# Moving one transform behind the sines, two products behind the next unit, and the last evictions onto two engines, in a kernel of attention and a state-space convolution

## The chip, the core and the metric

The kernel runs on one core of one Trainium2 chip. The core has a matrix engine (TensorE, PE in the profile, whose weight loads are listed as PEld), a vector engine (VectorE, DVE), an engine for casts and functions such as sine and exp (ScalarE, ACT), a general engine (GpSimd, POOL) and one that mostly issues DMAs (SyncE, SP). Each works through its own queue in order, and they wait for each other on semaphores. The metric is the device time of one execution in microseconds (us). The kernel before takes 423.83 us (median of 3 runs, 423.25 to 425.2).

## What is computed

There are two independent halves, whose results stand side by side in an output of 2048 x 1280.

```
a: qkv = x @ wqkv            x 2048 x 640, 32 heads of 20
   logits[s, w] = q[s] . k[s - 2w] * 20**-0.5,   w = 0..7   (window of 8, dilation 2)
   a = softmax_w(logits) applied to v[s - 2w], then @ wo
b: K[d, l] = Re sum_n C[d,n] * exp(dt[d] * A[d,n] * l) * dt[d] * B[d,n]     d 640, n 192, l 2048
   y = irfft( rfft(u padded to 4096) * rfft(K padded to 4096) )[:2048]      per channel d
   b = y + u * Dskip
```

In the second half, A is complex, so the exponential is a real exponential times a cosine and a sine of angles.

## The kernel before, in words

The 640 channels of b are worked through in five chunks of 128 (c = 0 to 4, `NCH`), in the first loop of `body`. For a chunk ScalarE makes tables of real exponentials (`exps_chunk`, 40 activations, tile R) and, in two halves of the chunk, tables of sines (`trig_half`: TensorE makes phases in the PSUM tiles ps_ph, ScalarE evicts them as sines into TA and TX, 8 evictions for a half). VectorE multiplies them together for each half (`small_half`: tiles PG, Q and two X) and then, for each of the two units of a half, makes three large product tables Y (`y_form`). TensorE contracts Y with X over n (`kgen_unit`, PSUM tile ps_k) and ScalarE evicts the unit's part of K into Ksb. Y has four buffers, which Q shares, so a new Y can be written only when the matmuls of an older one are done. A chunk has two halves of two units, so 12 Y in all.

The convolution is done in the frequency domain. `fwd` is a forward transform in two steps of 64 matmuls each: the first step's results are cast by ScalarE in four pieces into A, the second step's in four pieces into Sg. It is called as `transform(c)` for K of a chunk, and as `fwd_u` for u, whose spectrum goes to DRAM (Sdram). `products` loads the spectrum of u twice (P1, and P2 with its halves exchanged) and multiplies both by K's spectrum on VectorE (line 379). `inverse_a` is the first inverse step: four pieces of matmuls (ps_ia) and casts into Z, then a store to Zdram. A, Sg, P1, P2 and Z of both transforms share three buffers in turn (tag "sp"). All PSUM tiles of these steps (ps_ph, ps_f, ps_ia) share three double banks (tag "bank2"). `times_d` multiplies u with Dskip (tile UD) after certain units.

Chunk c works on the spectral steps of chunk c - 1: it runs transform(c - 1), then the two sets of sines, its first half's units, products and the inverse of c - 1, u's transform for chunk c + 1, and its second half, during which the exponentials and first sines of chunk c + 1 are made. In the last chunk, projections of q and k for the attention take the free places. Then the attention follows: products, logits and softmax, and `av_step`, which multiplies v by the attention weights on VectorE and sums over channels on TensorE (ps_o); at its last window position ScalarE evicts the two ps_o tiles into o. `out_proj` returns eight pieces for each quarter q of the rows; each piece is five matmuls into ps_op, an eviction into ob, and after every second piece a DMA to the output.

The order on each engine is made by a planner, from the order of the program as priorities and its own times for instructions. Two calls tie it down. `keep_in_program_order(ins)` places an instruction behind the one traced just before it on its engine. `issue_after(ins)` places all instructions that a block traces on the engine of `ins` behind `ins`. In chunks 1 to 4 the second half's `small_half` is placed in this way behind the second product of `products`, and the products of chunks 1 to 4 are kept in program order.

## Time and profile before

| what | value |
|---|---|
| median of 3 runs | 423.83 us |
| the profiled execution, its own time | 423.71 us |
| its span, first to last instruction | 421.9 us |
| busy: TensorE, VectorE, ScalarE | 352.2, 378.0, 313.6 us |
| mean granted TensorE clock | 0.935 of full speed |
| Y products, line 324, 60 of them | 103.1 us, 1753 ns each |
| casts of the first and second transform step, 40 each | 37.8 and 37.7 us |
| the chain that ended last | the last 8 projection pieces: PE 5.96 us, then one eviction of 0.49 us |

A row of the profile's timeline gives the start, the length of a run of like instructions, engine and line, operation, output and input tiles with their shapes, how many there were, and in brackets how long the engine had stood idle before them and which engine's instruction ended that. A row of the waits names who waited, for whom, the total in us, the number of times and the longest. A row of a table of stretches gives the stretch, its length, and the busy time of TensorE, the weight loads, VectorE, ScalarE and GpSimd with their numbers of instructions, then the granted clock, the share of DMA time and the rate in GB/s. Lines 441 and 442 are helpers through which all matmuls and copies of the attention's end go.

### The profile page before, as it was taken

The numbers are of one execution on the slowest core, as the hardware profiler recorded it, in microseconds if no ns is written. First come the engines' busy times: TensorE is split into PE (matmuls) and PEld (weight loads), VectorE is DVE, ScalarE is ACT, GpSimd is POOL, SyncE is SP. The second block draws the span as 40 slices with busy tenths as digits, with TensorE's granted clock in tenths as the row PEclk, the third lists the DMA queues.
The fourth block names the chain that finished last, engine by engine and source line by source line (L and its number), as shares of the span: only waits on it lengthen the run. The fifth ranks groups of instructions, "written<-read, shape, count | busy, mean of one in ns | idle before, by whom it ended". The sixth has DMA issues, their size and how long they took to land. (4 is left out here: it accounts for less than half of the span.)

```text
span 421.9 us, 18968 instructions
## 1 busy us (share of the span) xinstructions
PE 352.2 (83%) x8693; PEld 259.8 (62%) x8693; DVE 378.0 (90%) x350; ACT 313.6 (74%) x578; POOL 42.9 (10%) x85
## 2 busy tenths in 40 slices
PE   1288779989987888878997799999899989879895
PEld 0267678877865678666785586555545666445453
DVE  8999997998988999899996989955987999999961
ACT  2988989889998999979998684423666644746662
POOL 8630000000000000000010000000000300412120
PEclk9975969989997999889897899999999999999999
DMA  5599003262233402424079941700040472897642
GB/s 146 177 223 170 5 2 129 90 202 68 101 149 108 101 30 103 167 89 103 28 272 216 247 106 42 281 3 3 2 101 2 141 148 80 240 228 227 174 117 90
DMA packets 45336, 51.76 MB, mean 123 GB/s; under 512 B 31488, under 2 KB 39168, under 8 KB 42568
## 3 DMA queue, kind: packets, MB, share of 16 engines
q1 hardware_dynamic: 41592, 41.35, 36.4%
q0 software_dynamic: 3520, 9.08, 7.2%
q8 instruction: 68, 1.11, 1.1%
q10 hardware_dynamic: 144, 0.12, 0.1%
q14 instruction: 12, 0.10, 0.1%
HBM read 28.08 MB, written 18.35 MB: 110 GB/s over the span
## 5 line engine op out<-in xcount | busy, mean ns | idle before, releaser
L324 DVE TENSOR_TENSOR Y<-PG 128x3072 bf16<-128x3072 bf16 x60 | 103.1, 1753 | 6.8 <-PE ps_k L342 6.6
L337 PE MATMUL ps_k<-Y,X 128*32 128x64 bf16 x1920 | 47.6, 239 | 9.7 <-issue 6.5
L270 PE MATMUL ps_ph<-LPC 128*64 128x256 bf16 x400 | 44.4, 323 | 13.4 <-DMA LPC<-lo 8.7
L342 PE MATMUL ps_k<-Y,X 64*32 64x64 bf16 x1920 | 44.9, 234 | 4.6 <-issue 4.6
L337 PEld LDWEIGHTS <-X 128*32 128x32 bf16 x1920 | 32.2, 117 | 20.0 <-issue 12.5
L365 ACT CAST Sg<-ps_f 128x1024 bf16<-128x1024 f32 x40 | 37.7, 1042 | 7.7 <-PE ps_f L364 7.7
L244 ACT ACTIVATE R<-LPC 128x192 bf16<-128x192 f32 x155 | 41.8, 389 | 0.0
L357 ACT CAST A<-ps_f 128x1024 bf16<-128x1024 f32 x40 | 37.8, 1038 | 1.2 <-PE ps_f L356 1.1
L342 PEld LDWEIGHTS <-X 64*32 64x32 bf16 x1920 | 30.0, 113 | 13.8 <-issue 6.4
L294 DVE TENSOR_TENSOR X<-R,TX 128x1536 bf16<-128x1536 bf16 x40 | 37.2, 952 | 0.0
L364 PE MATMUL ps_f<-A,T 128*64 128x128 bf16 x640 | 25.3, 244 | 12.5 <-ACT A L357 10.5
L270 PEld LDWEIGHTS <-LPC 128*64 128x64 bf16 x400 | 21.5, 121 | 19.8 <-DMA LPC<-hi 8.8
L278 ACT ACTIVATE TX<-ps_ph 128x768 bf16<-128x768 int16 x40 | 30.4, 838 | 3.2 <-PE ps_ph L274 3.2
L364 PEld LDWEIGHTS <-T 128*64 128x64 bf16 x640 | 23.6, 127 | 14.3 <-issue 14.1
L630 DVE TENSOR_TENSOR prod<-v,atp 128x2048 bf16<-128x2048 bf16 (+2 forms) x32 | 30.8, 1018 | 0.7 <-PE ps_o L441 0.7
L274 PE MATMUL ps_ph<-LPC 128*64 128x128 bf16 x400 | 30.7, 249 | 0.0
L278 ACT ACTIVATE TA<-ps_ph 128x768 bf16<-128x768 int16 x40 | 29.8, 824 | 0.9 <-PE ps_ph L274 0.8
L274 PEld LDWEIGHTS <-LPC 128*64 128x64 bf16 x400 | 25.8, 131 | 1.1
L441 PE MATMUL ps_op<-wo,o 128*128 128x320 bf16 x160 | 23.9, 299 | 1.8 <-ACT ysb L442 0.9
L294 DVE TENSOR_TENSOR PG<-R,TA 128x3072 bf16<-128x3072 bf16 x10 | 17.5, 1752 | 8.0 <-ACT TA L278 8.0
L379 DVE TENSOR_TENSOR P<-P,Sg 128x4096 bf16<-128x4096 bf16 x10 | 22.9, 2287 | 2.0 <-DMA P<-Sdram 1.6
L543 DVE TENSOR_TENSOR prod<-qT,kT 128x1024 bf16<-128x1024 bf16 (+1 forms) x16 | 23.0, 1482 | 0.5 <-ACT qT L511 0.5
(135 smaller groups left out, 667.3 us busy)
## 6 DMA issues: line engine op xcount, KB each, us to landing
Sdram<-Sg SPq DMA_DIRECT2D x5, 1024.0 KB
P<-Sdram SPq DMA_DIRECT2D x5, 1024.0 KB
P<-Sdram SPq DMA_DIRECT2D x10, 512.0 KB
Zdram<-Z SPq DMA_DIRECT2D x5, 1024.0 KB
Z<-Zdram SPq DMA_DIRECT2D x30, 128.0 KB
U<-in_B_u_dram SPq DMA_DIRECT2D x4, 640.0 KB
UDdram<-UD SPq DMA_DIRECT2D x10, 256.0 KB
out_dram<-ysb SPq DMA_DIRECT2D x32, 80.0 KB
```

Source lines behind the costliest of these rows:

```text
L244: nc.scalar.activation(out=RX[:, :, e - 16, :], in_=src, func=ACT.Exp, scale=m)
L270: MM(o[64 * hh:64 * hh + 64, :, 0:8], lhsT=L[:, 64 * hh:64 * hh + 64], rhs=rhs, start=first, stop=last, skip_group_check=True, tile_positi ...
L274: MM(o[64 * hh:64 * hh + 64, :, 8:12], lhsT=L[:, 128:192], rhs=rhs[:, :, 16 * hh:16 * hh + 16], start=False, stop=last, skip_group_check=T ...
L278: last = nc.scalar.activation(out=dst, in_=words.rearrange("p b (q e f) -> p b q (e f)", e=8, f=4), func=ACT.Sin, scale=PI_LO / 32768.0)
L294: TT = lambda o, a, b, op: V.tensor_tensor(out=o, in0=a, in1=b, op=op)
L324: nc.vector.tensor_tensor(out=Y[:].rearrange("p q (b a) f -> p q b a f", a=8), in0=fa, in1=gb, op=A.mult)
L337: MM(ps[32 * g:32 * g + 32, t], lhsT=X[:, q, k, :, f], rhs=Ys[k][:, q, :, f], start=(t == 0 and k == 0), stop=False, tile_position=(0, 32 ...
L342: MM(ps[32 * g:32 * g + 32, t], lhsT=X[hb, q, k, :, f], rhs=Ys[k][hb, q, :, f], start=False, stop=(k == 2), tile_position=(64 * (g // 2), ...
L357: nc.scalar.copy(out=A1[:, :, 32 * b:32 * b + 32].rearrange("p k (j g) -> p k j g", g=4), in_=ps[:].rearrange("p j k g -> p k j g"))
L364: last = MM(ps[sl, kk], lhsT=C["T2"][:, 8 * b + kk, sl], rhs=A1[:, 8 * b + kk, :], start=(kk % 4 == 0), stop=True, skip_group_check=True, ...
L365: nc.scalar.copy(out=Sg[:, :, 8 * b:8 * b + 8, :], in_=ps[:].rearrange("p k (j g) -> p j k g", g=4))
L630: ins = nc.vector.tensor_tensor(out=p2.rearrange("p (d i) -> p d i", i=ni), in0=self.v2[:, 4 * j0:4 * j0 + 4 * nj, off:off + ni], in1=at[: ...
```

## The change

Four places of the program are edited.

- `fwd_u` for chunk c + 1 is called in chunks 1, 2 and 3 after the first sines of chunk c + 1, where it was called before the second half of chunk c. In chunk 0 it stays where it was.
- `products` and all four pieces of `inverse_a` are called after the second unit of the first half. Before, the products and the inverse's first piece stood between the two units and the other three pieces behind the second.
- The last `av_step` evicts its two ps_o tiles in four pieces, ScalarE and VectorE taking one half of each, where ScalarE took two whole ones.
- The last two pieces of the third quarter's projection are evicted by VectorE, and their store goes over SP. In the last quarter every second piece is evicted by VectorE as before, now tied to the program's order, and five of its eight pieces take PSUM from the double banks.

```diff
-    def av_step(self, i0, ni, j0, nj, w):
+    def av_step(self, i0, ni, j0, nj, w, last=False):
...
             for f, p in enumerate(self.ops):
-                self.copy(out=self.o4[:, j0:j0 + nj, 2 * f:2 * f + 2, i0:i0 + ni], in_=p[:, :, 0:n].rearrange("p s (j i) -> p j s i", i=ni))
+                for s in range(2) if last else ():
+                    (self.copy, self.vcopy)[s](out=self.o4[:, j0:j0 + nj, 2 * f + s, i0:i0 + ni], in_=p[:, s, 0:n].rearrange("p (j i) -> p j i", i=ni))
+                if not last:
+                    self.copy(out=self.o4[:, j0:j0 + nj, 2 * f:2 * f + 2, i0:i0 + ni], in_=p[:, :, 0:n].rearrange("p s (j i) -> p j s i", i=ni))
+
+    def vcopy(self, out, in_):
+        self.tc.keep_in_program_order(self.nc.vector.tensor_copy(out=out, in_=in_))
...
-        ps = self.one("ps_op")[:, 0:320]
+        if wide:
+            ps = self.big("ps_ow")[:, 0, 0:320] if (2 * sc + eh) % 5 < 3 else self.one("ps_op")[:, 0:320]
+        else:
+            ps = self.one("ps_op")[:, 0:320]
...
-            nc.vector.tensor_copy(out=ob[:, 320 * eh:320 * eh + 320], in_=ps)
+            self.vcopy(out=ob[:, 320 * eh:320 * eh + 320], in_=ps)
...
-        return [(lambda sc=sc, eh=eh: self.out_piece(q, sc, eh, last and eh == 1)) for sc in range(4) for eh in range(2)]
+        return [(lambda sc=sc, eh=eh: self.out_piece(q, sc, eh, eh == 1 if last else q == 2 and sc == 3, last)) for sc in range(4) for eh in range(2)]
...
         unit(c, 0, 0, F, G, Xs[0])
+        unit(c, 0, 1, F, G, Xs[1])
         if c > 0:
             P1, P2, last = products(tc, pools, Sk[c - 1], Sd[c - 1], fp, True)
-            ia = inverse_a(tc, pools, C, P1, P2, Zd[c - 1], fp)
-            ia[0]()
-        unit(c, 0, 1, F, G, Xs[1])
-        if c > 0:
-            for f in ia[1:]:
+            for f in inverse_a(tc, pools, C, P1, P2, Zd[c - 1], fp):
                 f()
-        if c < LAST:
-            last_u = fwd_u(tc, pools, C, Sd, c if c == 0 else c + 1)
-            if c == 0:
-                first_u = last_u
+        if c == 0:
+            first_u = fwd_u(tc, pools, C, Sd, 0)
...
             trig[c + 1, 0] = trig_half(tc, pools, B, c + 1, 0)
+            if c > 0:
+                fwd_u(tc, pools, C, Sd, c + 1)
...
-            att.av_step(i0, ni, j0, nj, w)
+            att.av_step(i0, ni, j0, nj, w, 8 * group + w == 47)
```

More of the change, by code (lines that the diff above doesn't have):

```diff
@@ L640, in av_step, with out_piece @@
             for f, p in enumerate(self.ops):
-                self.copy(out=self.o4[:, j0:j0 + nj, 2 * f:2 * f + 2, i0:i0 + ni], in_=p[:, :, 0:n].rearrange("p s (j i) -> p j s i", i=ni))
-    def out_piece(self, q, sc, eh, vec):
+                for s in range(2) if last else ():
[4 more added lines that the diff above has]
+        self.tc.keep_in_program_order(self.nc.vector.tensor_copy(out=out, in_=in_))
+    def out_piece(self, q, sc, eh, vec, wide=False):
         nc = self.nc
```

## The prediction

> **What bounds the kernel now.** I read the engines' shares first, then the stretches from one chunk's first VectorE instruction to the next one's, then the waits, then the timelines of VectorE, ScalarE, TensorE and the SP queue around them, and last the end of the run.
>
> ```profile
> PE 352.2 (83%) x8693; PEld 259.8 (62%) x8693; DVE 378.0 (90%) x350; ACT 313.6 (74%) x578; POOL 42.9 (10%) x85
> ...
> 74.30:128.05 53.75, 48.44 (x1521) 41.34 (x1519) 49.07 (x40) 50.41 (x95) 0.62 (x2) 0.94 0.37 124
> 128.05:178.04 49.99, 41.86 (x1214) 34.66 (x1210) 48.93 (x39) 47.25 (x92) 0.62 (x2) 0.94 0.28 96
> 178.04:230.05 52.01, 43.61 (x1280) 35.76 (x1278) 47.84 (x39) 47.46 (x91) 1.77 (x2) 0.89 0.52 147
> ...
> DVE PG L294 <- ACT TA L278: 8.0, 3, 4.0
> DVE Y L324 <- PE ps_k L342: 6.6, 4, 2.5
> ```
>
> VectorE leads, but the columns of the stretches of chunks 1, 2 and 3 (length, then TensorE, weight loads, VectorE, ScalarE) show three engines close together: 48.93 us of VectorE and 47.25 of ScalarE in a chunk of 49.99, and 41.86 of TensorE. A wait taken from one engine can go only as far as the next one lets it. VectorE's waits there are of two kinds: the new chunk's first product waits for the sines (8.0 us in three chunk changes), and the table product Y waits until TensorE has freed one of four Y buffers.
>
> ```profile
> 88.00 5.10 DVE L324 TENSOR_TENSOR Y<-PG 128x3072 bf16<-128x3072 bf16 x3
> 93.01 2.29 DVE L379 TENSOR_TENSOR P<-P,Sg 128x4096 bf16<-128x4096 bf16 x1
> 97.09 1.76 DVE L324 TENSOR_TENSOR Y<-PG 128x3072 bf16<-128x3072 bf16 x1 [1.78 <-PE ps_k L342]
> ...
> 128.05 1.76 DVE L294 TENSOR_TENSOR PG<-R,TA 128x3072 bf16<-128x3072 bf16 x1 [2.90 <-ACT TA L278]
> ```
>
> ```profile
> 108.33 3.80 ACT L357 CAST A<-ps_f 128x1024 bf16<-128x1024 f32 x4
> ...
> 112.97 3.76 ACT L365 CAST Sg<-ps_f 128x1024 bf16<-128x1024 f32 x4
> ...
> 125.05 2.92 ACT L278 ACTIVATE TA<-ps_ph 128x768 bf16<-128x768 int16 x4
> ...
> 132.87 3.80 ACT L357 CAST A<-ps_f 128x1024 bf16<-128x1024 f32 x4
> ```
>
> The first block shows both waits of chunk 1, and that the first spectral product P (2.2 us from start to start) fills part of the second. The second block is ScalarE: the casts of u's transform (108.33 and 112.97, about 7.5 us) stand ahead of the sines at 125.05, so the sines are 7.5 us later than they need be. The four casts at 132.87 begin the transform of the previous chunk's K. These casts stand at 82.86, 132.87, 183.91 and 236.38; I call them the anchors of chunks 1 to 4.
>
> **Part 1, u's transform behind the sines.** Nothing is added: 64 + 64 matmuls, 8 casts and one store of 1 MB move, once in each of chunks 1, 2 and 3. Before it, the sines come about 7.5 us sooner, against waits of 2.90, 1.06 and 4.04, so all 8.0 us of waiting for sines goes. That is the upper end. What is late next: the 8 casts now stand between the sines and the casts of K's transform, and the 128 matmuls among the six Y products' matmuls of the chunk's second half.
>
> **Part 2, products behind the second unit.** The two P are now tied behind the last Y of the first half (and its u times D), and the second half is tied behind them. So nothing fills a wait for a Y buffer. With TensorE as timed before: in chunk 1 VectorE is free at 93.1 and waits to 97.09, 4.0 in place of 1.78, so 2.2 are lost. In chunk 2 the fourth Y would end at 145.1 and wait for the first buffer:
>
> ```profile
> 145.50 0.41 PE L342 MATMUL ps_k<-Y,X 64*32 64x64 bf16 x15
> 145.84 0.68 PE L337 MATMUL ps_k<-Y,X 128*32 128x64 bf16 x32
> ```
>
> The matmuls that free it end at 145.84, 13.0 after the anchor; those that free the second end 2.3 later. In chunk 3 the first is freed 13.0 after 183.91 too. So the sixth Y ends no sooner than anchor + 13.0 + 2.3 + 1.7 = anchor + 17.0, and with u times D (1.25) and two P (4.4) the second half begins at anchor + 22.65. What VectorE gained at the sines it loses here, unless the anchors move as well.
>
> **How far the anchors move.** Three paths lead from one anchor to the next. VectorE: 48.9 of work. ScalarE: from 132.87 to the table load at 173.74 are 40.9; less 7.4 for u's casts and 1.0 for waits that exps can fill gives 32.5; table load 1.3, sines 5.8, then A 3.8, a gap of 0.8 (as at 137.45), Sg 3.8 and two copies of K 1.0 make 49.0. TensorE: second half at 22.65, its first Y ready 11.15 later (154.05 to 165.2), then six groups of Y matmuls at 1.2, five pairs of sine matmuls at 0.45, u's 3.8 + 2.2, and 1.5 of waiting for nothing shown (1.50 and 1.25 in two chunks), 16.95 in all, and 1.05 to the cast: 51.8 if all is in series; 49.4 if the last two Y groups (2.4) come behind u's transform, which K's first three casts need not wait for. Between 49.0 and 51.8 I take 50.0, nearest to the two lower paths, since K's casts need all four units only at the fourth.
>
> Chunk 1 by hand: second half at 97.09 + 1.7 + 1.2 + 4.4 = 104.4 (102.18 before); last VectorE instruction 22.97 later, so the next chunk starts at 127.4, against 128.05. ScalarE: sines 7.5 earlier, at 117.5, end 123.4, then u's casts and copies to about 132.7, the new anchor of chunk 2. From there 182.7 and 232.7, against 183.91 and 236.38: a lead of 3.7 at chunk 4. VectorE agrees: second half of chunk 3 at 182.7 + 22.65 = 205.35, the next chunk 21.9 later at 227.3, against 230.05.
>
> **The SP queue in chunk 4.** The last store of u's spectrum is moved past the loads of x.
>
> ```profile
> 220.32 0.32 SPq L416 DMA_DIRECT2D Sdram<-Sg  x1
> ...
> 222.78 14.69 SPq L451 DMA_TRANSPOSE xT<-in_A_x_dram  x4
> 237.57 0.52 SPq L375 DMA_DIRECT2D P<-Sdram  x1
> ```
>
> Those loads hold the queue 14.7 us, and start when u's buffer is free, that is after u's first matmuls, about 223.5. The store, ready near 230, leaves at 238, and the load of P takes the stored buffer. P's loads, issued at 237.57, had landed when P ran at 245.93 (it waited 0.43 for a cast), so they take at most 8.4; the store ahead of them, as large as the first, is bounded by 0 and as much again. P can then be used between 246.4 and 254.8, and VectorE wants it at 232.7 + 17.0 = 249.7: a cost of 0 to 5.1 there, while TensorE has k's projections to do. I take 1.2, from the middle of the two (250.6) and the hand-over: 3.7 − 1.2 makes **the middle −2.5**, with bounds −5.9 (no wait anywhere: 127.4 + 48.93 + 47.84 = 224.2 against 230.05) and +5 (the slow rival below). After that the same work runs in the same order, so this carries to the end.
>
> **Part 3, the last evictions.**
>
> ```profile
> 410.03 1.93 ACT L442 CAST o<-ps_o 128x1024 bf16<-128x1024 f32 x2
> 411.84 0.77 ACT L442 CAST ob<-ps_op 128x320 bf16<-128x320 f32 x2
> 412.33 5.95 PE L441 MATMUL ps_op<-wo,o 128*128 128x320 bf16 x40 [0.89 <-ACT ob L442]
> ```
>
> Two casts of 1024 become four of 512. ScalarE's half costs 0.53 each (two took 1.07 at 402.20); VectorE shows no such cast: bounded by 0.49 (320 wide) below and 1.0 (ScalarE's 1024) above, I take 0.7, so the four end at 411.4 instead of 411.96. The two following evictions and their DMA go to VectorE and SP, both idle then. With PSUM tiles of its own the last projection follows the one that ends at 411.45, not 412.33: **−0.9**. Its 40 matmuls in 5.95 still pace the end, so wider PSUM brings no more. Bounds 0 and −0.9: even at 1.0 each VectorE's two casts would end at 412.05, before 412.33, so a loss is excluded.
>
> **Sum.** −2.5 − 0.9 = −3.4 from the profiled execution's 423.71 (span 421.9 and 1.8 around it): **420.3**. The median of 423.83 differs by 0.1, which I leave.
>
> **Rivals.** *No wait takes the place:* VectorE alone bounds, −5.9 − 0.9: 416.9. For it: planner and engines had slack at each anchor (2.11 of TensorE). Against: ScalarE's 49.0.
> *The wait only changes its name:* Y buffers take back what the sines gave, anchors as before, 423.71 − 0.9 = 422.8. For it: anchor + 17.0 lies beyond VectorE's arrival in every chunk from 2 on.
> *Slower, TensorE's queue:* matmuls keep their order, so Y groups stand behind u's second matmuls, which stand behind casts. Fully in series a chunk takes 51.8. With a halved clock it is more: the granted clock shows 0.50 from 125 to 131 after a hole of 1.50, where a sine pair took 0.78, not 0.45, and a second transform (64) 3.36, not 2.17; 5 × 0.33 + 1.2 add 2.85: 54.65. Taking u's matmuls out of 158.7 to 165.2 leaves TensorE, with the coefficients' and the first sine matmuls, some 2.6 busy of 6.5 there, where now it is 5.81 busy at clock 1.00, so the hole is made by this change. Midway, 53.2 a chunk with chunk 1's end at 135.0, the last anchor is 241.4, 5.0 late: 423.71 + 5.0 − 0.9 = 427.8. It decides from a last anchor of about 239.4, where the loss passes 0.5%.
> The Trainium skill's page "TensorE: Matmul & The Clock Gate", section "Part 1: The HAM clock gate", says that an idle window of about 3.4 us halves the clock and as much work restores it; by that rule the hole of 4 us halves it for 3.4 us in each chunk, by estimate four sine pairs at 0.33 more, 51.3 a chunk, 423.0 in the end, which is where the wait that changes its name lies. The trace agrees on the halving, not on the size: 1.50 of hole was enough, and it lasted 6 us and more.
>
> **How the numbers follow.** Chances: my forecast 0.40 (its own range 418.5 to 422), no wait 0.16, changed name 0.18, slower 0.26. The range takes in the no-wait case below and most of the slow one above: 416.5 to 427. About 0.5% (2.1 us) is what a measurement here tells from no change: faster than that, 0.34 of the forecast and all of the no-wait case, 0.50; within it, 0.06 and the changed name, 0.24; slower 0.26.
>
> **What would show it.** Right: no wait of PG for TA; VectorE's waits for Y buffers in the first halves of chunks 1 to 4 at 4.0 and then 1 to 2 each; anchors 50 apart, the last near 232.7; the last projection starting when the one before it ends. Wrong: anchors 52 or more apart with TensorE at half clock in the second half; or P waiting for its load in chunk 4 by more than 1.3.

## The result, and the profile after

The changed kernel takes 443.03 us (median of 4 runs, 441.21 to 444.83); the kernel before took 424.51 us beside it (423.25 to 428.24). The ratio is 1.0397, with a 95% interval of 1.0336 to 1.0458: the change makes the kernel 4% slower, where 420.3 was forecast. The profiled execution took 441.92 us, with a span of 440.1. Here and below, executions of a program over 1.5% slower than its fastest are left out of the ratios but not of the medians, so that a ratio can differ from that of two medians by some tenths of a per cent.

The first block has the engines' shares in the changed kernel, the second three rows of its table of waits, the third the last two of these rows in the kernel before.

```profile
PE 357.5 (81%) x8693; PEld 266.9 (61%) x8693; DVE 380.0 (86%) x354; ACT 314.5 (71%) x576; POOL 46.5 (11%) x84
```

```profile
DVE Y L324 <- PE ps_k L342: 33.1, 11, 6.2
ACT Ksb L343 <- PE ps_k L342: 24.0, 13, 4.7
...
PE ps_k L337 <- DVE Y L324: 13.6, 9, 4.3
```

```profile
ACT Ksb L343 <- PE ps_k L342: 13.0, 10, 3.6
...
PE ps_k L337 <- DVE Y L324: 3.2, 5, 1.5
```

VectorE has the same work as before (380.0 us against 378.0) in a longer span. Its 8.0 us of waiting for sines are gone without a trace, and its waiting for Y buffers has grown from 6.6 to 33.1 us. ScalarE waits 24.0 us for the units of K where it waited 13.0. In both rows the engine waited for is TensorE, and TensorE itself waits 13.6 us for Y, where it waited 3.2.

The stretches from one chunk's first VectorE instruction to the next one's, for chunks 1, 2 and 3, with the columns as before (length, TensorE, weight loads, VectorE, ScalarE, GpSimd, granted clock, DMA share, GB/s):

```profile
74.26:126.80 52.54, 42.96 (x1261) 35.87 (x1258) 48.99 (x41) 47.92 (x92) 0.62 (x2) 0.87 0.29 98
126.80:187.95 61.15, 49.94 (x1412) 42.62 (x1411) 49.24 (x40) 51.97 (x96) 0.62 (x2) 0.83 0.26 85
187.95:245.60 57.65, 44.44 (x1277) 37.66 (x1272) 47.93 (x40) 47.25 (x91) 1.78 (x2) 0.82 0.38 124
```

Chunk 1 is 1.2 us shorter than before, chunks 2 and 3 are 11.2 and 5.6 longer, at a granted clock of 0.83 and 0.82 where it was 0.94 and 0.89. No engine is busy more than 52 us in the 61: in chunk 2 they wait for each other in turn. The anchors (the four casts that begin the transform of the previous chunk's K) show where:

| anchor of chunk | 1 | 2 | 3 | 4 | steps |
|---|---|---|---|---|---|
| before | 82.86 | 132.87 | 183.91 | 236.38 | 50.0, 51.0, 52.5 |
| forecast | 82.86 | 132.7 | 182.7 | 232.7 | 50 each |
| after | 82.86 | 136.07 | 193.38 | 253.60 | 53.2, 57.3, 60.2 |

Each step falls into a first half (from the anchor to the second half's first VectorE instruction, PG) and a second (from there to the next anchor):

| chunk | first half before, after | second half before, after |
|---|---|---|
| 1 | 19.3, 21.1 | 30.7, 32.1 |
| 2 | 21.2, 23.9 | 29.9, 33.5 |
| 3 | 20.2, 26.3 | 32.3, 34.0 |

The first halves lost 10.5 together, the second halves 6.7. The last anchor is 17.2 late, and chunk 4's own first half is 2.6 longer (23.2 against 20.7); the last product of the attention on VectorE ends 19.9 late (427.87 against 407.93), and the span is 18.2 longer, so the end of the run gives 1.7 back.

The timeline of VectorE in chunk 2, then that of TensorE and that of ScalarE in the second half of that chunk:

```profile
149.39 1.76 DVE L324 TENSOR_TENSOR Y<-PG 128x3072 bf16<-128x3072 bf16 x1 [4.40 <-PE ps_k L342]
152.62 1.76 DVE L324 TENSOR_TENSOR Y<-PG 128x3072 bf16<-128x3072 bf16 x1 [1.47 <-PE ps_k L342]
...
159.92 1.75 DVE L294 TENSOR_TENSOR PG<-R,TA 128x3072 bf16<-128x3072 bf16 x1
...
185.04 1.76 DVE L324 TENSOR_TENSOR Y<-PG 128x3072 bf16<-128x3072 bf16 x1 [4.77 <-PE ps_k L342]
```

```profile
171.21 0.69 PE L337 MATMUL ps_k<-Y,X 128*32 128x64 bf16 x32 [2.81 <-DVE Y L324]
...
174.77 0.64 PE L270 MATMUL ps_ph<-LPC 128*64 128x256 bf16 x4 [2.46 <-ACT TA L278]
...
179.63 2.00 PE L356 MATMUL ps_f<-BD,U 128*64 128x128 bf16 x32
...
185.82 1.53 PE L364 MATMUL ps_f<-A,T 128*64 128x128 bf16 x48
...
192.66 1.47 PE L356 MATMUL ps_f<-BD,Ksb 128*64 128x128 bf16 x45
```

```profile
180.83 3.05 ACT L357 CAST A<-ps_f 128x1024 bf16<-128x1024 f32 x3 [0.56 <-PE ps_f L356]
184.18 1.01 ACT L357 CAST A<-ps_f 128x1024 bf16<-128x1024 f32 x1 [0.30 <-PE ps_f L356]
186.50 3.76 ACT L365 CAST Sg<-ps_f 128x1024 bf16<-128x1024 f32 x4 [1.31 <-PE ps_f L364]
190.12 0.63 ACT L343 CAST Ksb<-ps_k 128x512 bf16<-128x512 f32 x1
192.78 0.59 ACT L343 CAST Ksb<-ps_k 128x512 bf16<-128x512 f32 x1 [2.04 <-PE ps_k L342]
```

This is the second half in order of time, with the rows on which it turns. The first Y comes at 171.2, after TensorE had stood for 2.81. Then TensorE's queue is blocked for 2.46 by sine matmuls that wait for a PSUM bank, with Y matmuls behind them. Then u's first step, between scraps of Y matmuls; u's second step; the remaining Y matmuls; and only behind the last of these, at 192.66, the first matmul of K's transform. In the kernel before u's 128 matmuls ran from 158.9 to 166.9, ahead of the first Y's matmuls at 168.8.

### The profile page after: what moved, and what is told of

It is laid out like the page before. It is cut to its first block, busy times and chain, and to the rows that moved or that the text cites. A ratio compares the mean times of both kernels' runs of the same rounds, so it can differ in the third digit from the quotient of the medians.

```text
span 440.1 us, 18965 instructions
## 1 busy us (share of the span) xinstructions
PE 357.5 (81%) x8693; PEld 266.9 (61%) x8693; DVE 380.0 (86%) x354; ACT 314.5 (71%) x576; POOL 46.5 (11%) x84
## 5 line engine op out<-in xcount | busy, mean ns | idle before, releaser
L324 DVE TENSOR_TENSOR Y<-PG 128x3072 bf16<-128x3072 bf16 x60 | 103.2, 1754 | 33.1 <-PE ps_k L342 33.1
L337 PE MATMUL ps_k<-Y,X 128*32 128x64 bf16 x1920 | 48.2, 239 | 24.1 <-DVE Y L324 13.6
L270 PE MATMUL ps_ph<-LPC 128*64 128x256 bf16 x400 | 45.4, 331 | 15.6 <-DMA LPC<-lo 7.8
L270 PEld LDWEIGHTS <-LPC 128*64 128x64 bf16 x400 | 22.8, 125 | 21.0 <-issue 8.6
L364 PE MATMUL ps_f<-A,T 128*64 128x128 bf16 x640 | 27.3, 256 | 7.3 <-ACT A L357 6.0
L364 PEld LDWEIGHTS <-T 128*64 128x64 bf16 x640 | 25.4, 135 | 9.1 <-issue 8.5
L343 ACT CAST Ksb<-ps_k 128x512 bf16<-128x512 f32 x20 | 11.7, 587 | 24.0 <-PE ps_k L342 24.0
L274 PEld LDWEIGHTS <-LPC 128*64 128x64 bf16 x400 | 26.9, 134 | 0.8
L492 PE MATMUL ps_k<-xT,wkq 128*128 128x512 bf16 x100 | 22.4, 379 | 0.3 <-ACT Sg L365 0.3
```

The source lines that it names most:

```text
L270: MM(o[64 * hh:64 * hh + 64, :, 0:8], lhsT=L[:, 64 * hh:64 * hh + 64], rhs=rhs, start=first, stop=last, skip_group_check=True, tile_positi ...
L274: MM(o[64 * hh:64 * hh + 64, :, 8:12], lhsT=L[:, 128:192], rhs=rhs[:, :, 16 * hh:16 * hh + 16], start=False, stop=last, skip_group_check=T ...
L324: nc.vector.tensor_tensor(out=Y[:].rearrange("p q (b a) f -> p q b a f", a=8), in0=fa, in1=gb, op=A.mult)
L337: MM(ps[32 * g:32 * g + 32, t], lhsT=X[:, q, k, :, f], rhs=Ys[k][:, q, :, f], start=(t == 0 and k == 0), stop=False, tile_position=(0, 32 ...
L364: last = MM(ps[sl, kk], lhsT=C["T2"][:, 8 * b + kk, sl], rhs=A1[:, 8 * b + kk, :], start=(kk % 4 == 0), stop=True, skip_group_check=True, ...
```

## The experiments

Three theories are named in the expectations. A: it is the place of u's transform, in the one queue that TensorE has. B: it is the place of the products, which no longer fill VectorE's waits for Y buffers. C: it is the granted clock, halved by the holes that the change makes. Each ratio is against the kernel before, run beside it on the same chip.

| run | ratio | 95% interval |
|---|---|---|
| u's transform moved alone | 1.0167 | 1.0111 to 1.0224 |
| products and inverse moved alone | 1.0263 | 1.0200 to 1.0326 |
| last evictions alone | 0.9950 | 0.9912 to 0.9989 |
| all, u's transform behind the third unit | 1.0266 | 1.0189 to 1.0342 |
| all, hole filled with matmuls | 1.0315 | 1.0233 to 1.0397 |
| all, products not tied | 1.0266 | 1.0177 to 1.0354 |
| u alone, last store over GpSimd's queue | 1.0256 | 1.0167 to 1.0346 |
| u behind K's transform, and last evictions | 1.0747 | 1.0665 to 1.0829 |
| half of u's transform, and last evictions | 1.0018 | 0.9981 to 1.0055 |
| before, without u's transform | 0.9848 | 0.9786 to 0.9910 |
| all, without u's transform | 1.0112 | 1.0059 to 1.0164 |
| inverse's first piece moved alone | 1.0005 | 0.9960 to 1.0050 |
| u in chunks 1 and 2 alone | 1.0152 | 1.0120 to 1.0184 |
| half of u and last evictions, last store over GpSimd's queue | 0.9988 | 0.9944 to 1.0031 |

### One part at a time

```diff
-        if c < LAST:
-            last_u = fwd_u(tc, pools, C, Sd, c if c == 0 else c + 1)
...
+            if c > 0:
+                fwd_u(tc, pools, C, Sd, c + 1)
```

> Only u's transform is moved behind the sines; the products stay between the two units and the end is as before. Theory A (TensorE's queue: the second half's Y matmuls stand behind u's transform, and K's transform starts late in every chunk): most of the loss of 18 us is here, 435 to 443 us, anchors 53 to 60 us apart, and the sixth Y of a second half waits 4 to 5 us. Theory B (the products behind the second unit leave Y's waits unfilled, and the transform alone is a gain): 417 to 423 us, no wait for sines, anchors near 50.

Measured: 435.46 us, 1.67% slower, with anchors at 83.36, 133.43, 188.67 and 243.09 (steps 50.1, 55.2, 54.4). TensorE in chunk 2 of this run:

```profile
166.44 0.68 PE L337 MATMUL ps_k<-Y,X 128*32 128x64 bf16 x32 [0.71 <-DVE Y L324]
...
168.97 0.67 PE L337 MATMUL ps_k<-Y,X 128*32 128x64 bf16 x32 [1.27 <-DVE Y L324]
...
171.31 0.64 PE L270 MATMUL ps_ph<-LPC 128*64 128x256 bf16 x4 [1.22 <-ACT TA L278]
...
176.89 1.18 PE L356 MATMUL ps_f<-BD,U 128*64 128x128 bf16 x16
...
187.94 1.57 PE L356 MATMUL ps_f<-BD,Ksb 128*64 128x128 bf16 x48
```

The first Y matmuls are early (166.4, before 168.8), and K's first matmul is 4.7 late (187.94, before 183.19), with u's 128 matmuls between the two. The move alone costs time, and in A's range. A's signs are there in part: the first step is 50.1, not 53 or more, and the longest waits of a Y in a second half are 2.37 and 3.30, not 4 to 5.

```diff
         unit(c, 0, 0, F, G, Xs[0])
-        if c > 0:
-            P1, P2, last = products(tc, pools, Sk[c - 1], Sd[c - 1], fp, True)
...
         unit(c, 0, 1, F, G, Xs[1])
+        if c > 0:
+            P1, P2, last = products(tc, pools, Sk[c - 1], Sd[c - 1], fp, True)
```

> Only the products and the inverse step are moved behind the second unit; u's transform stays before the second half and the end is as before. Theory A: a small loss, the 2.2 us per chunk that no longer fill a wait, in part given back by the wait for the sines: 424 to 429 us. Theory B: most of the loss, 434 us or more.

Measured: 439.36 us, 2.63% slower; anchors at 83.11, 133.96, 188.59 and 244.91 (steps 50.9, 54.6, 56.3). VectorE's rows in chunk 2:

```profile
149.53 1.76 DVE L324 TENSOR_TENSOR Y<-PG 128x3072 bf16<-128x3072 bf16 x1 [0.25 <-PE ps_k L342]
151.21 1.31 DVE L408 TENSOR_TENSOR UD<-U,Dsb 128x1024 bf16<-128x1024 bf16 x1
152.43 4.49 DVE L379 TENSOR_TENSOR P<-P,Sg 128x4096 bf16<-128x4096 bf16 x2
156.83 1.76 DVE L294 TENSOR_TENSOR PG<-R,TA 128x3072 bf16<-128x3072 bf16 x1
...
177.63 3.43 DVE L324 TENSOR_TENSOR Y<-PG 128x3072 bf16<-128x3072 bf16 x2 [2.46 <-PE ps_k L342]
```

The second half begins at the anchor + 22.9 (156.83), as the forecast had it (22.65), and 1.7 later than before (21.2). But it doesn't stay at 1.7: the inverse follows the second P, u's transform follows the inverse, and a Y in the second half then waits 2.46 more. Both parts cost, so neither A nor B is the whole.

```diff
+                for s in range(2) if last else ():
+                    (self.copy, self.vcopy)[s](out=self.o4[:, j0:j0 + nj, 2 * f + s, i0:i0 + ni], in_=p[:, s, 0:n].rearrange("p (j i) -> p j i", i=ni))
```

> Only the end is changed: the last evictions on two engines and the last projection's own PSUM tiles. Both theories: a gain of 0.9 us by the prediction's sum, 1.4 us by the trace of the changed kernel (the last 50 projection matmuls in 6.97 us, where before the last 50 with the gap in them took 8.36): 422.4 to 423.3 us. If the gain is not there in the median, the end was paced by something else, 423.8.

Measured: 426.14 us (12 runs) against 426.57, a ratio of 0.995 with an interval that ends at 0.9989: about 2 us faster by the ratio, though the medians differ by 0.4 only. By the ratios it is the fastest version with the full computation that was run. The three parts add up to 1.67 + 2.63 − 0.50 = 3.8%, against 3.97% of the whole change.

### Where u's transform goes

```diff
-            if c > 0:
-                fwd_u(tc, pools, C, Sd, c + 1)
...
             unit(c, 1, 0, F, G, Xs[0])
-        if c == 0:
-            fwd_u(tc, pools, C, Sd, 1)
+        if c < LAST:
+            fwd_u(tc, pools, C, Sd, c + 1)
```

> The changed kernel, but u's transform is called one unit later, behind the third unit of a chunk instead of ahead of it, so only the fourth unit's matmuls can stand behind it. Theory A: the wait of the sixth Y in the second half (4.8 and 4.1 us) goes or shrinks below 2, and the time falls by a third to two thirds of the loss, 428 to 437 us. Theory B: the products still stand behind the second unit, so the time stays near 441 to 443.

This edit is made in the changed kernel. Measured: 439.14 us, a ratio of 1.0266; steps 52.5, 55.8 and 54.9, the last anchor 7 earlier than with the whole change. The waits of 4.8 and 4.1 of the second halves' Y are gone (0.83 and 1.64 are left). With the third unit's Y matmuls ahead of u's, a third of the loss is given back, with intervals that just touch: at the same work, the place in TensorE's order seems to count. The anchors put it lower: the three second halves are 3.0 shorter than with the whole change, while 4.0 are gained in chunk 3's first half, which this edit doesn't touch.

```diff
-            P1, P2, last = products(tc, pools, Sk[c - 1], Sd[c - 1], fp, True)
+            P1, P2, last = products(tc, pools, Sk[c - 1], Sd[min(c - 1, 1)], fp, True)
...
-        if c < LAST:
-            last_u = fwd_u(tc, pools, C, Sd, c if c == 0 else c + 1)
...
```

The edit shown is that of the kernel before; the second run makes the same one in the changed kernel.

> The kernel before without u's transform in chunks 1 to 3; the products of the later chunks read the spectrum of chunk 1's u in its place. This measures the price of these three transforms in their old place. Theory A: they fill a hole of TensorE, and only ScalarE's casts ahead of the sines cost, so the waits for sines (2.90, 1.06 and 4.04) go and nothing else: about 416 to 418 against 425. If TensorE were the bound there too, the price is nearer to three times 8.5, and the time 400 to 410.

> The changed kernel without u's transform in chunks 1 to 3, with the spectrum of chunk 1's u in its place: the price of the three transforms in their new place. Theory A (TensorE's queue in the second half): without them the second half has only Y and sines, the steps between anchors fall from 53.2, 57.3 and 60.2 to 50 or 51, and the time to 421 to 427, so the price is 16 to 22, twice that of the old place. Theory B (waits for Y buffers in the first half, products no longer filling them): the waits of 3.6 to 6.3 in the first halves stay and the time is 430 to 435, a price of about 8 to 13.

Measured: 422.72 us and 433.03 us against 427.60. Leaving u's three transforms out makes the kernel before 1.5% faster (some 6.5 us) and the changed kernel 2.85% (1.0397 to 1.0112, some 12 us). So the same 384 matmuls and 24 casts cost nearly twice as much in the changed kernel, by the middles of the intervals. Without them the changed kernel is still 2.6% above the kernel before without them (1.0112 − 0.9848), although it has the last evictions' gain of 0.5%: that is the price of the products again, some 3%, free of u's transform, and on B's side of the second expectation. Rows of the changed kernel without u:

```profile
199.50 1.76 DVE L324 TENSOR_TENSOR Y<-PG 128x3072 bf16<-128x3072 bf16 x1 [3.18 <-PE ps_k L342]
...
230.29 3.43 DVE L324 TENSOR_TENSOR Y<-PG 128x3072 bf16<-128x3072 bf16 x2 [2.54 <-PE ps_k L342]
```

The first is the wait of chunk 3's first half that no P fills, the second one of its second half, behind Y and sines alone; the steps are 47.4, 52.8 and 58.2, not 50 or 51 as A expected. (In the 58.2 TensorE also stood for 2.58 and 3.16 in the midst of groups. The timeline names nothing that it waited for; the last section says what such stands go with.) In the first of the two runs the waits for sines were gone, and the gain of 1.5%, with an interval of 0.9 to 2.1%, reaches what A expected of it (1.6 to 2.1%).

```diff
         if c > 0:
             transform(c - 1)
+            if c < LAST:
+                fwd_u(tc, pools, C, Sd, c + 1)
...
-        if c < LAST:
-            last_u = fwd_u(tc, pools, C, Sd, c if c == 0 else c + 1)
...
```

> The kernel before, with the last evictions of the change, and u's transform in chunks 1 to 3 right behind the transform of K, ahead of the sines of the second half; the products stay between the units. Theory A (what counts is which hole of TensorE u's matmuls fill): they fill the hole beside the casts of K's transform (TensorE was idle 2.1 and 0.8 of 7 us there), the second half keeps nothing but Y and sines, the steps between anchors come to about 50, and the time is 419 to 423. Rival (ScalarE bounds there): the 8 casts stand ahead of the second half's sines, which end at 154.5 in place of 146.9 against a VectorE that asks for them at 154.05, and the four exponentials behind come late too; waits for sines of 1 to 4 in each chunk, and 427 or more.

Measured: 456.57 us, 7.5% slower. It is slower, as the rival had it, but for another cause than either account gave. VectorE waits 29.8 us for the loads of P, up to 8.7 at a time, where it hardly waited for them before. By the code, A, Sg, P1, P2 and Z take three buffers in turn, and with u's A and Sg ahead of P1 and P2 a load of P must wait until u's spectrum is stored. So A could not be judged by this run.

### Which wait carries part 2

```diff
-            P1, P2, last = products(tc, pools, Sk[c - 1], Sd[c - 1], fp, True)
+            P1, P2, last = products(tc, pools, Sk[c - 1], Sd[c - 1], fp, False)
```

> The changed kernel, but the spectral products are no longer kept in program order on VectorE, so that the first product stands ahead of the sixth Y again and can fill the wait for a Y buffer; the inverse stays behind the second unit, and u's transform behind the sines. Theory B (the waits for Y buffers that P no longer fills are the loss of part 2): the waits of the first halves fall by 1.5 to 2.2 in each of four chunks, the second halves start that much sooner, the steps between anchors fall by about 2 each, and the time falls from 443 to 435 or 437. Theory A (TensorE's queue in the second half sets the anchors): the wait only moves to the second half's Y or to the next anchor, and the time stays within 2 of 443.

This one is made in the changed kernel too. Measured: 437.54 us, a ratio of 1.0266 against 1.0397 of the change. VectorE's rows in chunk 2:

```profile
144.14 2.29 DVE L379 TENSOR_TENSOR P<-P,Sg 128x4096 bf16<-128x4096 bf16 x1
148.68 1.76 DVE L324 TENSOR_TENSOR Y<-PG 128x3072 bf16<-128x3072 bf16 x1 [2.24 <-PE ps_k L342]
```

With one P ahead of the fifth Y the wait is 2.24, not 4.40, and the time falls by 1.3%, at the edge of what B expected and with intervals that just overlap. The three first halves are 2.2, 2.1 and 5.3 shorter than with the whole change and come to 61.6 in all, near the 60.7 of the kernel before. B had the steps fall by about 2 each; they are 52.7, 57.0 and 53.9, since the second halves grow by 2.4 (102.0 against 99.6) and most of the gain is in chunk 3, whose first half in the changed kernel has a stand of TensorE that this run lacks (196.71, shown further down). In chunk 4 P then waits 5.58 for its load. So the tie makes the first halves long, as B says, but a part of what they give back is lost again elsewhere.

```diff
-            ia[0]()
         unit(c, 0, 1, F, G, Xs[1])
         if c > 0:
-            for f in ia[1:]:
+            for f in ia:
```

> The kernel before with the products left between the two units, tied as before, and only the first piece of the inverse called behind the second unit with the other three. Theory B (the loss of part 2 is that the products no longer fill VectorE's waits for Y buffers): VectorE's order is that of the kernel before, so the time stays within 2 us of it, 425 to 429. Rival, theory D (the loss of part 2 is the place of the inverse's matmuls: behind all Y groups of the first half instead of between them, so that u's transform and the next sines come later): the steps between anchors grow by 2 or more as in the run of the products alone (50.9, 54.6, 56.3), and the time is 432 or more.

Measured: 428.17 us against 428.56, a ratio of 1.0005. The inverse's place by itself is free, so D falls. What part 2 loses begins with the products' leaving the waits, which is B; how much of it are the waits themselves, and how much the inverse and u's transform that come late behind the products, wasn't measured.

### The clock

```diff
     ps = pools["psum"].tile([128, 8, 64], f32, name="ps_k", tag="bank", bufs=2)
+    for i in range(warm):
+        MM(ps[:].rearrange("p t a -> p (t a)"), lhsT=pools["T2"][:, 0, :], rhs=pools["T2"][:, 4:8, :].rearrange("p a b -> p (a b)"), start=True, stop=True, skip_group_check=True)
```

> The changed kernel with 12 matmuls of 512 columns without any use in chunks 1 to 3, in TensorE's queue just ahead of the third unit's matmuls; they write the PSUM tile that the third unit overwrites. In chunk 2 TensorE had no work there from 168.4 to 171.2, and its granted clock was 0.50 from 170.5 to 180. At full clock the 12 take about 2.6 us. Theory C (the halved clock carries a good part of the loss): the granted clock of the stretches rises from 0.82 to 0.9 or more, sine pairs of the second half take 0.45 in place of 0.78, the steps between anchors fall from 53.2, 57.3 and 60.2 by 2.5 to 3 each, and the time falls from 443 to about 435. Theory A (the order of TensorE's queue carries it, whatever the clock): the steps fall by less than 1 each, and the time stays at 440 to 445.

Measured: 439.14 us, a ratio of 1.0315; steps 52.4, 55.6 and 55.65. The stretch from the second half's first VectorE instruction to the next anchor, for chunks 2 and 3, first of the changed kernel and then of this run; after them TensorE's rows of this run:

```profile
159.92:193.38 33.46, 27.70 (x727) 23.93 (x725) 28.42 (x25) 27.63 (x54) 0.62 (x2) 0.80 0.20 79
219.65:253.60 33.95, 26.97 (x725) 23.19 (x725) 29.71 (x28) 27.29 (x53) 1.78 (x2) 0.83 0.60 151
```

```profile
158.73:190.66 31.93, 29.82 (x767) 24.63 (x767) 27.79 (x25) 27.65 (x53) 0.62 (x2) 0.95 0.18 70
213.15:246.31 33.16, 27.85 (x711) 22.72 (x713) 30.43 (x29) 26.40 (x51) 1.77 (x2) 0.93 0.62 151
```

```profile
168.50 2.76 PE L334 MATMUL ps_k<-T 128*128 128x512 bf16 x12
171.20 0.68 PE L339 MATMUL ps_k<-Y,X 128*32 128x64 bf16 x32
...
174.31 0.41 PE L270 MATMUL ps_ph<-LPC 128*64 128x256 bf16 x4 [1.85 <-ACT TA L278]
```

The 12 matmuls fill the hole to the microsecond (168.50 to 171.2) and the clock is at 0.95 and 0.93 in place of 0.80 and 0.83. The steps fall by 0.8, 1.7 and 4.6, the time by about 0.8% (some 3.5 us), with intervals that overlap. So C's share is about a fifth at the measured size, and not clear of noise. Of the 7.1 in the steps the second halves, which the filling is meant for, have 3.1 (0.8, 1.5 and 0.8); 3.8 are in chunk 3's first half. At nearly full clock the second halves still take 31.9 and 33.2 (29.9 and 32.3 before) and the last two steps 55.6: the rest of the loss is there at full clock.

### The SP queue in chunk 4

```diff
-    tc.nc.sync.dma_start(out=Sd[c], in_=Su[:].rearrange("p a b c -> p (a b c)"))
+    (tc.nc.gpsimd if c == NCH - 1 else tc.nc.sync).dma_start(out=Sd[c], in_=Su[:].rearrange("p a b c -> p (a b c)"))
```

> The kernel before with only u's transform moved, as in the first experiment, but the last store of u's spectrum goes over GpSimd's queue, so that it doesn't stand behind the loads of x on SP. If that queue is what made the product P wait 7.37 and 0.85 in chunk 4, both waits fall below 1.5 and the time falls from 435.5 to 428 or 430, leaving the anchors' 4.2 and 1.9. If the wait is only what VectorE had left over because TensorE (k's projections and the Y matmuls) was late anyway, a wait of P or Y for another engine takes its place and the time stays at 433 to 436.

Measured: 435.31 us, a ratio of 1.0256 against 1.0167 without this edit, no gain. P in chunk 4 still waits 6.83 (7.37 without this edit). Its load stands behind the loads of x on SP, and these begin only when u's first step has read u's buffer: at 232.3 in this run, 222.8 in the kernel before. So the run didn't tell the two causes apart. The next one takes the queue out of it. It too is the kernel before with u's transform moved alone.

```diff
+            if c in (1, 2):
+                fwd_u(tc, pools, C, Sd, c + 1)
```

> The kernel before with u's transform moved behind the sines in chunks 1 and 2 only; in chunk 3 it stays in its old place, so that u's buffer is free for the loads of x, and the store of u's spectrum done, as early as before. Theory A (TensorE's queue: the anchors of chunks 3 and 4 slip by 4.2 and 1.9 in the run with all three moved): the slip of 4.2 at chunk 3's anchor stays, chunk 3 can take back at most the 4.0 that VectorE waits for sines there, and the time is 430 to 433 against 427. Theory Q (most of part 1's loss arises in chunk 4, where the loads of x start when u's last transform has read its buffer, and P's load stands behind them and behind the store): without it P waits less than 1.5 in chunk 4, and the time is within 2 of the kernel before, 425 to 429.

Measured: 434.35 us, a ratio of 1.0152; steps 50.1, 55.2 and 55.2. P in chunk 4 doesn't wait at all, and the loss is nearly that of all three chunks, so theory Q's "within 2 of the kernel before" falls. The step from chunk 2's anchor, with u's transform moved there, is 55.2 as in the first experiment. But the next step is 55.2 too (52.5 before), though u's transform stood in its old place there. In that chunk VectorE waited 7.26 for sines, whose matmuls stood behind this row of TensorE, while the loads of x ran:

```profile
236.73 0.62 PE L337 MATMUL ps_k<-Y,X 128*32 128x64 bf16 x28 [4.99 <-issue]
```

The timeline names nothing that these matmuls waited for ("issue"); the stand ends right behind a transfer of instructions, as the last section shows, and the longest such stand of the kernel before was 1.99. So the run shows TensorE's queue at work in chunk 2, and leaves open what the third step would have been without this stand.

```diff
-            last_u = fwd_u(tc, pools, C, Sd, c if c == 0 else c + 1)
+            A_u = fwd_u_a(tc, pools, C, c + 1)
...
+                fwd_u_b(tc, pools, C, Sd, c + 1, A_u)
```

> The kernel before, with the last evictions of the change, and u's transform of chunks 1 to 3 cut in two: its first step (64 matmuls and 4 casts into A) stays where it was, its second step (64 matmuls, 4 casts into Sg and the store) goes behind the sines of the next chunk. Theory A (it counts which hole of TensorE u's matmuls fill): the first step still fills TensorE's hole and frees u's buffer for the loads of x as before, the sines come 3.75 sooner, and of the waits of 2.90, 1.06 and 4.04 at most 0.3 is left; the second half has 2.2 us of matmuls more, at full clock; steps between anchors 49 to 51 and 417 to 421 in all. Rival (any matmul of u between the second half's Y and K's transform goes straight to the anchors, with its casts): the steps grow by 2 to 3 each against 50.0, 51.0 and 52.5, as VectorE's waits for sines become waits for Y buffers, and the time is 427 to 431.

Measured: 428.24 us, a ratio of 1.0018; anchors at 84.64, 134.47, 186.36 and 237.15, so the steps are 49.8, 51.9 and 50.8. All waits for sines are gone, and from anchor 1 to anchor 4 it takes 152.5 against 153.5 before. In chunk 4 the SP queue shows at last:

```profile
224.75 15.13 SPq L473 DMA_TRANSPOSE xT<-in_A_x_dram  x4
239.98 0.52 SPq L431 DMA_DIRECT2D Sdram<-Sg  x1
245.99 0.32 SPq L387 DMA_DIRECT2D P<-Sdram  x1
```

```profile
251.16 2.29 DVE L391 TENSOR_TENSOR P<-P,Sg 128x4096 bf16<-128x4096 bf16 x1 [4.69 <-ACT TA L278]
```

The store leaves behind the loads of x, the load waits for it, and P is used at 251.16 after a wait of 4.69. K's Sg was ready at 248.1, so 3 us of that can be the queue's.

```diff
-    tc.nc.sync.dma_start(out=Sd[c], in_=Su[:].rearrange("p a b c -> p (a b c)"))
+    (tc.nc.gpsimd if c == NCH - 1 else tc.nc.sync).dma_start(out=Sd[c], in_=Su[:].rearrange("p a b c -> p (a b c)"))
```

> The run with only the second step of u's transform moved, and its last store over GpSimd's queue. In that run the store left SP at 239.98, behind the loads of x, P's load into the stored buffer followed at 245.99, and P waited 4.69 until 251.16; K's Sg, which P needs too, was ready at 248.1. If SP's queue is what that run lost in chunk 4, the store lands before the loads of x end, P's wait falls from 4.7 to 1.7 or less, and the time falls by 3, from 428.2 to about 425, a ratio of 0.995 against 1.002. If TensorE sets the pace there (holes of 2.1 and 1.2 ahead of K's casts in chunk 4, while the loads of x run), or the store takes longer beside the loads of x, the wait stays or changes its name, and the ratio stays at 1.000 to 1.005.

Measured: 427.52 us, a ratio of 0.9988 (0.9944 to 1.0031) against 1.0018 (0.9981 to 1.0055). The difference of 0.3% lies inside both intervals, so this one is inconclusive, and no version with u's transform moved, whole or in part, is shown to beat the last evictions alone.

## Why the prediction was wrong

**Part 1's gain was right, and was spent.** All 8.0 us of waiting for sines went. In chunk 1 the sines start at 117.45 (117.5 forecast) and the next chunk at 126.80 (127.4 forecast).

**Part 2 in chunk 1 was right.** The wait for a Y buffer is 3.55 (4.0 forecast), and the second half begins at 103.93 (104.4 forecast).

**The step that failed is "How far the anchors move".** It set three paths beside each other, 48.9 for VectorE, 49.0 for ScalarE, 51.8 for TensorE in series, put 49.4 beside the last for the case that two Y groups come behind u's transform, and took 50.0 as nearest to the lower ones. The reason given, that K's casts need all four units only at the fourth, didn't come into play: in chunk 2 K's first matmul (192.66) stands behind every Y matmul and behind all of u's, so TensorE runs the half in series. TensorE's rows of the kernel before have that order already, right behind the last Y matmuls of chunk 2:

```profile
182.59 0.66 PE L342 MATMUL ps_k<-Y,X 64*32 64x64 bf16 x32
183.19 2.42 PE L356 MATMUL ps_f<-BD,Ksb 128*64 128x128 bf16 x64
```

The first anchor behind the change already shows it: 132.7 was forecast from ScalarE's casts, and ScalarE, done with the sines at 124.5, got to K's casts only at 136.07, as K's matmuls began at 135.35. The series path was in the text, as a rival with a chance of 0.26, and was rated too low. The sign that the text names for being wrong at this step came too: anchors 52 or more apart, with TensorE at half clock in the second half. The range, 416.5 to 427, was said to take in most of that rival; its own middle, 427.8, lies outside.

**That path was undersized too.** It gave 51.8, or 54.65 at half clock, and the steps are 53.2, 57.3 and 60.2. Three terms were short. The second half begins at anchor + 23.9 in chunk 2 and + 26.3 in chunk 3, not + 22.65: in chunk 3, K's casts were themselves split by 1.74, behind a stand of TensorE of 2.58 (the row below; the last section says what it goes with). The sines in the second half block TensorE's queue for 2.46 (1.85 at full clock), which no term held. And u's casts wait for u's matmuls, which wait for the sines' PSUM banks: the sum had TensorE and ScalarE each in its own series, never one waiting for the other.

```profile
196.71 0.75 PE L356 MATMUL ps_f<-BD,Ksb 128*64 128x128 bf16 x19 [2.58 <-issue]
```

**The half clock was priced too high.** The rival had 2.85 a chunk, 8.55 in the three; filling the hole shortened the three second halves by 3.1 in all. The 7.1 by which the steps fell would fit the price, but by chance: 3.8 of them are in chunk 3's first half, where the changed kernel's profile has the stand of 2.58 and the run with the hole filled has none like it. The Trainium skill's page "TensorE: Matmul & The Clock Gate", section "Part 1: The HAM clock gate", has the clock halved after an idle window of about 3.4 us and restored by as much work. The trace agrees that work in the hole is the remedy: 2.76 us of matmuls took the stretch from 0.80 to 0.95. It doesn't agree on the size: a stand of 2.81 with little work ahead of it left the clock at 0.50 from 170.5 to about 180.

**The wait that changes its name** was the right mechanism for part 2 with the wrong end: the Y buffers took back what the sines had given, and then went on taking. The sums of the three first and the three second halves show which part loses where:

| run | first halves | second halves |
|---|---|---|
| before | 60.7 | 92.8 |
| the whole change | 71.2 | 99.6 |
| u's transform moved alone | 61.6 | 98.1 |
| products and inverse moved alone | 67.2 | 94.6 |
| all, u's transform behind the third unit | 66.7 | 96.5 |
| all, hole filled with matmuls | 67.3 | 96.5 |
| all, products not tied | 61.6 | 102.0 |

The products alone cost 6.5 in the first halves and 1.8 in the second, u's transform alone 0.9 and 5.3. The whole change lost 10.5 in the first halves, some 4 more than the products alone. Three of these 4 are in chunk 3's first half, 26.3 there against 22.2 to 23.3 with the products alone, with u's transform behind the third unit, or with the hole filled. That half has the stand of 2.58, and so has the changed kernel without u's transform (2.58 as well, the half 26.1), while those three runs don't; whether the change brings it about stays open. In the run of the products alone the sum is 11 to 13 us, where 2.2 were worked out for chunk 1 and nothing was added for the later chunks once the anchors were taken at 50.

**The SP queue** was bounded by 0 to 5.1 with 1.2 taken. In the changed kernel it cost nothing, as VectorE came later than the load. Where VectorE came in time, P was used at 251.16, inside the 246.4 to 254.8 of the text.

**Part 3 was right in sign and short in size.** From the start of the last ps_o matmuls to the end of the last eviction it takes 9.54 before (409.33 to 418.87) and 8.07 after (429.05 to 437.12): 1.47 in place of 0.9. The rows of TensorE and one of VectorE after:

```profile
429.63 1.53 PE L441 MATMUL ps_op<-wo,o 128*128 128x320 bf16 x10
431.00 2.20 PE L441 MATMUL ps_ow<-wo,o 128*128 128x320 bf16 x15
433.04 1.52 PE L441 MATMUL ps_op<-wo,o 128*128 128x320 bf16 x10
434.40 2.20 PE L441 MATMUL ps_ow<-wo,o 128*128 128x320 bf16 x15
```

```profile
430.36 1.29 DVE L647 CAST o<-ps_o 128x512 bf16<-128x512 f32 x2 [2.49 <-ACT o L442]
```

VectorE's casts of 512 took 0.65 each (0.7 taken). The last 40 matmuls take 5.6 from 431.00, where they took 5.95, so the wider PSUM did bring something, against what the text said. (By the edit and by these rows six of the last quarter's eight pieces, 30 of the 40 matmuls, use it, not five.)

## What to carry to other kernels

Where three engines are within a few per cent of each other, a wait that goes on one of them is worth what the in-order queue of the next one lets through, so follow the moved matmuls in that queue past every group that will stand behind them, and let the series sum lead unless a row shows that two groups can swap. A product that fills a wait, or a transform that fills a hole, is already cheap: here the same transform cost 6.5 us where it filled a hole and 12 where it didn't, and the products cost 2.6% once they had left the waits. Work moved out of a hole also leaves TensorE idle there, which here went with half the clock for the next 10 us; filling the hole gave back about a fifth of the loss, which isn't clear of noise. And a stretch that is longer in one profile can hold a stand that need not come from the move, so compare the stretch over several runs before its length is put down to the move.

## What the runs showed of the hardware

At a granted clock of 0.50 the groups of 64-column Y matmuls took 0.69 for 32 (171.21), as at full clock (0.68), while sine matmuls and transform steps, with 128 and 256 columns, slowed: a first group of 4 sine matmuls took 0.64 in place of 0.41, and the 64 matmuls of K's second step took 3.63 at 0.50 (199.03) where two groups of 48 and 16 took 1.53 and 0.64 at full clock in the kernel before (136.72). Which matmuls stand behind a hole decides what the clock costs.

TensorE also stood still in the midst of a group, with "issue" in the timeline in place of an engine that it waited for: 2.58 between two parts of K's first step in chunk 3 of the changed kernel, 2.72 and 2.42 in chunk 4 of the run with the store elsewhere and 4.99 in chunk 3 of the run with u moved in two chunks, where the loads of x were under way, and 5.55 in chunk 4 of the run with u behind the third unit, where the queue was past them; the longest such stand in the kernel before, in chunks 1 to 4, was 2.0. The traces have one thing beside nearly all of these stands. The DMA view lists a queue of its own for instructions, with transfers of 16 KB, about 40 between 75 and 300 us. In the 16 profiles 117 "issue" stands of TensorE in that stretch are 0.9 or longer, and 115 of them end 1.2 to 1.6 us after such a transfer has ended:

| run | TensorE stands | transfer of instructions | from its end to the next matmul |
|---|---|---|---|
| before | 225.55 to 227.54 | 225.06 to 226.07 | 1.47 |
| the whole change | 194.13 to 196.71 | 194.31 to 195.24 | 1.47 |
| u in chunks 1 and 2 alone | 231.74 to 236.73 | 234.24 to 235.34 | 1.39 |
| all, u's transform behind the third unit | 264.42 to 269.97 | 267.42 to 268.68 | 1.29 |

So TensorE had most likely run out of instructions there, and the long stands are those in which the transfer began late: 2.5 and 3.0 us into the stands of 4.99 and 5.55, but ahead of the stand of 1.99. What makes a transfer begin late wasn't tried and stays open, and with it whether the change brings the stand of 2.58 about.
